# A fused spectral and MLP block on one core: block products in a fourth group, x added earlier, one subtraction moved to GpSimd

## The chip, the core and the metric

The kernel runs on one core of a Trainium2 chip. The metric is the device time of one execution, in microseconds; the time before is the median of three runs. Engines are named as the profile names them: PE (TensorE, matrix products; PEld are its weight loads), DVE (VectorE), ACT (ScalarE), POOL (GpSimd) and SP (SyncE, which here issues all the DMAs).

## The reference

Input x is 2048 x 448 in 32-bit floats. Three things are summed:

```python
xn = layernorm(x)
A  = irfft2(rfft2(xn) * (w_r + 1j * w_i))          # spectral filter, over tokens and channels
h  = gelu(xn @ w1)                                 # 448 x 448
hs = concat(h[:, quarter k] shifted by 1, -1, 2, -2 tokens) @ w2
x1 = x + hs
B  = x1 + gelu(layernorm(x1) @ w3) @ w4            # 448 x 1792, 1792 x 448
out = x + A + B
```

So x itself enters the output twice: once as the leading `x +`, once inside x1.

## The kernel before, in words

Products run in 16-bit halves: a 32-bit operand is split into a high half and a low half (the rest), and a product is three matmuls: high by high, high by low, low by high. The 2048 tokens form 16 batches of 128 (token = 16 a + b, batch b). Tile `xb(b)` holds a batch: first the normalised x, then x1 divided by the scale p12, and in the end the output.

The stages, in order of the span:

- Start (to about 113 us): loads, layernorm, first MLP products (`w1_in`, L462; `w2_mm`, L507).
- Channel MLP, eight groups G of two batches, each in seven steps fp. `front(G, fp)` (L755) makes 256 hidden columns by 22 matmuls (`mlp_in`, L433) into a PSUM bank of tag `mm`; ACT applies gelu (L763) and writes the high half of `hf` (L767), DVE the low half (L768). `back(G, fp)` (L778) multiplies `hf` by w4 into the accumulators `acc` (L798). `mlp` (L837) strings them together, with `ahead` fronts issued before each back.
- Block products (`crossed`, L752; groups listed in `STR`, which is 5, 6, 7). For the two small products, high by low and low by high, `back` uses seven products of half width (224 columns, L809) in place of eight (four 448-column matmuls), as in Strassen's scheme. That needs differences of blocks: `hg`, three DVE operations (L771 to L773) with two buffers, and `w4_forms` (L890), made once on POOL. Partial sums go to two more banks `cr` (tag `tr`), are scaled by two ACT copies (L826), combined by four POOL additions (L829) and added to the batch by two more (L833; on DVE for group 7).
- Fold (`do_fold`, L568, two batches at a time, about 113 to 190 us): SP loads raw x into `xf` (three buffers), ACT normalises it in place (L575), POOL folds it (L580 to L583), `step1_in` (L588) splits it into `xh` (L591 on ACT, L592 on DVE), `step1` (L595) transforms it (ps, L601) and splits into `y` (L605, L606).
- The filter's largest value (`w_scale`, L610): eight loads `wl` and eight DVE reductions (L268), in two buffers.
- Spectral chunks (16, about 194 to 265 us): `chunk_a` (pp, L658), `chunk_b` (px, L675; two ACT copies L680; DVE products L681 and L683 into `te`; POOL addition L685 makes z), `chunk_z` (z split: high half on ACT, L692; low half on DVE, L693), `chunk_c` (pu, L704; `y`, L707 and L708).
- Inverse (`gather_u`, `inv_a`, `inv_b`, about 270 to 380 us): per batch pe (L724), an ACT copy, two POOL and four DVE operations, a split into `vh`, py (L746), then `xb += sc * py` on DVE (L747). `finish` (L560) calls `unscaled` (L553): it loads raw x again into `xr`, computes `p12 * xb + x` on DVE (L557), and stores. Batches 12 to 15 do this earlier, in `mlp(last=True)`, into tiles `rest` in the memory `x2mem` of which their fronts have no more need.

What sets the order of the work. A scheduler places the instructions of every engine at build time, by priority: the MLP runs under `prio(FILL)`, a low priority, so that it fills PE between the transforms, and its evacuations under `prio(EVAC)`, a high one. `behind(key)` pins an instruction behind another in that order: `FOLD` lists the (G, fp) whose `hf` each fold follows, `PACE` the (G, fp) whose `back` each step1 follows, `WMAX` those of the reductions. Each engine then runs its list strictly in order, and waits at an instruction whose inputs are not there. All DMAs stand in one list on SP. PSUM banks come in four tags of two (`mm`, `tr`, `acc`, `sp`); ps, px, pu, pe and py share `sp`.

Of the kernel before, what the change touches and what calls it, by code (L numbers as in the profile page):

```python
# [31 lines left out]
AH = 2  # L32
# [3 lines left out]
WMAX = [(1, 4), (1, 5), (2, 0), (2, 0), (2, 1), (2, 2), (2, 3), (2, 4)]  # L36
LATE = [(2, 2), (2, 3), (2, 4), (2, 5)]
HS = 3
STR = (5, 6, 7)
INV, LAG = 4, 2  # L40
EVAC, FILL = 0, 100000

# [80 lines left out]
def body(tc, nc, x, wf, w1, w2, w3, w4, c_g, c_n, c_small, out):  # L123
# [434 lines left out]
        return t  # L558

    def finish(b):  # L560
        SY.dma_start(ov[:, b], unscaled(b))


    OFF = [0, 113, 225, 338, 450]
    FAM = [0, 2, 1, 3]
    folds = {}

    def do_fold(b0):  # L568
        f = pfd.tile([128, 2, 4, 113], F32, tag="xf", bufs=3, name=f"xf{b0}")
        X = f.rearrange("p b s d -> p (b s d)")[:, 0:2 * D + 2].rearrange("p (b d) -> p b d", b=2)  # L570
        after["X", b0] = (SY.dma_start(X[:, :, 0:D], xv[:, b0:b0 + 2]).ins,)
        with behind("f", *FOLD[b0 // 2]):
            for i in range(2):
                x_ = X[:, i, 0:D]
                A.activation(out=x_, in_=x_, func=AF.Identity, scale=xn_scale[b0 + i], bias=xn_bias[b0 + i])  # L575
            A.activation(out=X[:, :, D:D + 1], in_=X[:, :, 0:1], func=AF.Copy)
        ad = X[:, :, 0:D].rearrange("p b (h d) -> p h b d", h=2)[:, :, :, 0:113]
        bc = X[:, :, 1:D + 1].rearrange("p b (h d) -> p h b d", h=2)[:, ::-1, :, 223:110:-1]
        u = xr.rearrange("p (a b s d) -> p a b s d", a=2, b=2, s=2)
        P.tensor_tensor(out=u[:, 0], in0=ad, in1=bc, op=ALU.add)  # L580
        P.tensor_tensor(out=u[:, 1], in0=ad, in1=bc, op=ALU.subtract)
        for k, op in ((0, ALU.add), (2, ALU.subtract)):
            i = P.tensor_tensor(out=f[:, :, k:k + 2].rearrange("p b s d -> p s b d"), in0=u[:, :, 0], in1=u[:, :, 1], op=op)  # L583
        after["fold", b0] = (i.ins,)
        for i in range(2):
            folds[b0 + i] = f[:, i].rearrange("p s d -> p (s d)")
# [33 lines left out]
    def w_scale_end(wm):  # L620
        t = pc.tile([128, 4], F32, name="wt")
        V.tensor_reduce(out=t[:, 0:1], in_=wm, axis=AX.X, op=ALU.max)
        pt = bank("sp", "wpt")
        T.transpose(pt[0:1, 0:128], t[:, 0:1], ident)
        V.tensor_reduce(out=t[0:1, 1:2], in_=pt[0:1, 0:128], axis=AX.X, op=ALU.max)
        V.tensor_scalar(out=t[0:1, 1:2], in0=t[0:1, 1:2], scalar1=2.0 ** -20, scalar2=None, op0=ALU.max)
        pb = bank("sp", "wpb")
        T.matmul(pb[:, 0:1], ones[0:1], t[0:1, 1:2], start=True, stop=True)
        e = pc.tile([128, 3], I32, name="we")
        V.tensor_copy(out=t[:, 2:3], in_=pb[:, 0:1])  # L630
        V.tensor_single_scalar(e[:, 0:1], t.bitcast(I32)[:, 2:3], 0x7F800000, op=ALU.bitwise_and)
        V.tensor_single_scalar(e[:, 1:2], e[:, 0:1], 0x7F800000, op=ALU.bitwise_xor)
        V.tensor_scalar(out=sc[:, 0:1], in0=e.bitcast(F32)[:, 1:2], scalar1=ZPRE, scalar2=None, op0=ALU.mult)
        for h in range(2):
            V.tensor_scalar(out=sc[64 * h:64 * h + 64, 2:3], in0=sc[64 * h:64 * h + 64, 0:1], scalar1=2.0 * h - 1.0,
                            scalar2=None, op0=ALU.mult)
        V.tensor_scalar(out=sc[:, 1:2], in0=e.bitcast(F32)[:, 0:1], scalar1=2.0 ** -21 / (ZPRE * UPRE * VPRE),
                        scalar2=s12[:, 0:1], op0=ALU.mult, op1=ALU.mult)


    stream, pfs, zs = {}, {}, {}
# [46 lines left out]
    def chunk_z(c):  # L688
        z = zs.pop(c)
        zh = zb[c % 2]  # L690
        zv = [zh[:, p * 2 * DF:(p + 1) * 2 * DF] for p in range(2)]
        A.activation(out=zv[0], in_=z, func=AF.Copy)  # L692
        V.tensor_tensor(out=zv[1], in0=z, in1=zv[0], op=ALU.subtract)  # L693

    def chunk_c(c):
        _, _, k = stream.pop(c)
# [45 lines left out]
    def inv_b(b):  # L742
        vh = vhs.pop(b)
        py = bank("sp", f"py{b}")
        for n, (vi, ri) in enumerate(PASS):
            T.matmul(py[:, :D], cV[ri], vh[:, vi], start=n == 0, stop=n == 2)  # L746
        V.scalar_tensor_tensor(out=xb(b), in0=py[:, :D], scalar=sc[:, 1:2], in1=xb(b), op0=ALU.mult, op1=ALU.add)  # L747


    acc, xs, hs, hg, rest = {}, {}, {}, {}, {}  # L750
# [27 lines left out]
    def back(G, fp):  # L778
        h = hs.pop((G, fp))
        n = D // 2  # L780
        end = 4 if G == 7 else 6
        if fp == 0:
            acc[G] = [bank("acc", f"acc{G}{i}") for i in range(2)]
            if G in STR:
                xs[G] = [bank("tr", f"cr{G}{i}") for i in range(2)]
        if (G, fp) == (7, 5):
            xs[G] = [bank("tr", f"end{i}") for i in range(2)]
        C = [[(slice(0, D), acc[G][i][:, 0:D], 0, 6)] for i in range(2)]
        if G == 7:
            C[1] = [(slice(0, D), acc[G][1][:, 0:D], 0, 4)]  # L790
            if fp > 4:
                C[1] = [(slice(n * k, n * k + n), xs[G][k][:, 0:n], 5, 6) for k in range(2)]
        for i in range(2):
            for r, to, s, e in C[i]:
                with behind("m", G, fp) if (G, fp) == (7, 6) and ("m", G, fp) in after else contextlib.nullcontext():
                    for f in range(2):
                        for hi, wi in ((0, 0),) if crossed(G, fp) else ((0, 0), (0, 1), (1, 0)):
                            m = T.matmul(to, h[:, hi, 2 * f + i], w4p[0][:, wi, 2 * fp + f, r],  # L798
                                         start=fp == s and f == 0 and hi + wi == 0, stop=fp == e and f == 1 and hi == 1)
                after["m", G, fp] = (m.ins,)  # L800
        if crossed(G, fp):
            g = hg.pop((G, fp))
            X = [xs[G][k // 2][:, n * (k % 2):n * (k % 2) + n] for k in range(4)]
            H = [[acc[G][i][:, n * k:n * k + n] for k in range(2)] for i in range(2)]
            forms = [(0, 1, X[0], 9), (1, 3, H[1][0], 9), (3, 2, H[0][0], C[0][0][3]), (6, 4, X[2], 9),
                     (4, 5, X[3], end), (5, 6, X[1], end), (2, 7, H[1][1], C[1][0][3])]
            for hi, wi in ((0, 1), (1, 0)):
                for k, slot, to, e in forms:
                    m = T.matmul(to, h[:, hi, slot] if slot < 4 else g[:, hi, slot - 4], w4f[fp][k][wi], start=k in (0, 6) and fp == 0 and hi == 0,  # L809
                                 stop=hi == 1 and fp == e)  # L810
            after["m", G, fp] = (m.ins,)
        k34 = p34[:, 1:2] if G >= 6 else p34[:, 0:1]
        to = {i: rest[2 * G + i] if G >= 6 else xb(2 * G + i) for i in range(2)} if fp >= 4 else {}

        def evacuate(i):
            for r, src, _, e in C[i]:
                if fp == e:
                    V.scalar_tensor_tensor(out=to[i][:, r], in0=src, scalar=k34, in1=to[i][:, r], op0=ALU.mult, op1=ALU.add)  # L818
                    if G == 7 and fp == 6:
                        SY.dma_start(ov[:, 2 * G + i, r], to[i][:, r])  # L820

        with prio(EVAC):
            if G in STR and fp == end:
                e0, e1 = cross[:, 0], cross[:, 1]
                for i in range(2):
                    A.activation(out=cross[:, i], in_=xs[G][i][:, 0:D], func=AF.Copy, scale=k34)  # L826
                for o, x, y in ((e0[:, n:], e0[:, 0:n], e0[:, n:]), (e1[:, 0:n], e1[:, 0:n], e0[:, n:]),
                                (e0[:, n:], e0[:, n:], e1[:, n:]), (e1[:, n:], e1[:, 0:n], e1[:, n:])):
                    (V if G == 7 else P).tensor_tensor(out=o, in0=x, in1=y, op=ALU.add)  # L829
            for i in range(2):  # L830
                evacuate(i)
                if G in STR and fp == end:
                    (V if G == 7 else P).tensor_tensor(out=to[i], in0=to[i], in1=cross[:, 1 - i], op=ALU.add)  # L833
                if G == 6 and fp == 6:
                    SY.dma_start(ov[:, 2 * G + i], to[i])
# [235 lines left out]
    xh_buf = [pfd.tile([128, 2 * 452 + 16], F16, name=f"xh{i}") for i in range(4)]  # L1071
    for i in range(4):
        P.memset(xh_buf[i][:, 904:], 0.0)
    mlp([1, 2], ahead=AH, tags=("mm", "tr"))
    for b in range(0, NB, 2):
        do_fold(b)
        step1_in(b)
        step1_in(b + 1)
        with behind("m", *PACE[b // 2]):
            step1(b)  # L1080
            step1(b + 1)
# [24 lines left out]
        if 0 <= i - 3 < NC:  # L1106
            chunk_c(i - 3)
    close("pst")
    mlp(range(3, 6))
    pv = pool("pv", side="right")  # L1110
    bs = [*range(12, 16), *range(8, 12), *range(8)]
    units = [(G, fp) for G in range(4, 8) for fp in range(7)][INV:]
# [11 lines left out]
                    finish(bs[n - 1])  # L1124

    inverse(range(4))
    mlp([6], last=True)
    inverse(range(4, 17))
    mlp([7], last=True)
    for name in ("pv", "pa2", "pa", "pw", "px", "pc", "ps"):  # L1130
# [25 lines left out]
```

## Time and profile before

| | us |
|---|---|
| runs (three) | 409.61, 410.98, 411.87; median 410.98 |
| the profiled execution, its own time | 411.11 |
| its span (first to last instruction) | 409.2 |
| PE busy | 402.4 |
| DVE busy | 313.3 |
| ACT busy | 268.2 |
| POOL busy | 164.1 |

Durations below come from the one profiled execution. A busy time counts an engine as busy from the start of an instruction to its end; matmuls are pipelined, so the time that one takes of PE is read from the distance between starts, not from its own duration. In the rows, "out<-in" names tiles of the program with buffer numbers left out, "x12" is a count, and what stands in brackets behind a row is the idle time of that engine just before it and what ended it.

### The profile page before, as it was taken

What the parts mean: (1) busy time and instruction counts of PE and PEld (TensorE: products, weight loads), DVE (VectorE), ACT (ScalarE), POOL (GpSimd) and SP (SyncE); (2) the same over time, 40 slices, a digit from 0 to 9 for tenths busy, and PEclk for the clock granted to TensorE, in tenths of its full rate; (3) what the DMA queues carried; (4) which work ended last, traced back from release to release, by engine and by line L of the source; (5) the groups of instructions that cost most, each with busy time, mean ns of one, the idle gap of its engine ahead of it and who ended that gap; (6) DMA issues with size and microseconds to landing.
All of it is one profiled execution on the core that took longest, in us unless ns stands there. A gap on an engine that the chain in (4) does not pass through costs nothing.

```text
span 409.2 us, 8827 instructions
## 1 busy us (share of the span) xinstructions
PE 402.4 (98%) x3379; PEld 295.4 (72%) x3379; DVE 313.3 (77%) x674; ACT 268.2 (66%) x465; POOL 164.1 (40%) x260
## 2 busy tenths in 40 slices
PE   8999999999999999999999999999999999999996
PEld 3554555666677877677878887877788888878885
DVE  5989998898654737975899988841698969898645
ACT  4699993984838766754788888757566555644332
POOL 3889820002297745599321212100133234434300
PEclk9999999999999999999999999999999999999999
DMA  8999999907710356527367567320000202332201
GB/s 280 352 264 181 170 178 259 270 2 156 159 48 0 94 207 198 158 24 179 94 173 157 144 149 181 98 60 2 1 2 2 69 22 77 107 108 76 88 2 45
DMA packets 57209, 49.46 MB, mean 121 GB/s; under 512 B 41312, under 2 KB 52192, under 8 KB 57168
## 3 DMA queue, kind: packets, MB, share of 16 engines
q1 hardware_dynamic: 57168, 48.91, 46.3%
q8 instruction: 26, 0.43, 0.4%
q14 instruction: 15, 0.12, 0.1%
HBM read 35.06 MB, written 3.67 MB: 95 GB/s over the span
## 4 chain that ended last, share of the span: by engine, by line
PE 68%; DVE 12%; ACT 7%; DMA 6%; issue 3%; POOL 1%; SPq 0%; ACTq 0%; DVEq 0%; POOLq 0%
PE pw L433 23%; PE acc L798 18%; PE pw L462 6%; PE pw L507 6%; PE cr L809 3%; DMA wl<-wf 2%; PE acc L809 2%; ACT te L680 2%; PE ps L601 2%; PE py L746 2%; PE pe L724 2%; DVE te L683 1%; DVE te L681 1%; PE pu L704 1%; DMA h<-hs 1%
## 5 line engine op out<-in xcount | busy, mean ns | idle before, releaser
L433 PE MATMUL pw<-x2mem,w3p 128*128 128x256 f16 x1232 | 151.4, 272 | 0.0
L433 PEld LDWEIGHTS <-w3p 128*128 128x128 f16 x1232 | 118.8, 98 | 18.4
L798 PE MATMUL acc<-w4p,hf 128*128 128x448 f16 x508 | 106.7, 352 | 0.2 <-DVE xt L818 0.2
L798 PEld LDWEIGHTS <-hf 128*128 128x128 f16 x532 | 51.6, 98 | 37.1 <-issue 0.4
L768 DVE SCALAR_TENSOR_TENSOR hf<-pw,h,hf 128x512 f16<-128x512 f32 x56 | 41.8, 747 | 35.3 <-ACT hf L767 35.0
L763 ACT ACTIVATE pw<-pw,pe 128x512 f32<-128x512 f32 x56 | 36.7, 655 | 42.5 <-PE pw L433 42.4
L731 POOL TENSOR_TENSOR e<-e 128x226 f32<-128x226 f32 x16 | 12.8, 801 | 72.0 <-ACT e L728 67.9
L767 ACT ACTIVATE hf<-pw,h 128x512 f16<-128x512 f32 x56 | 38.3, 685 | 1.3
L507 PE MATMUL pw<-w2p,h 112*128 112x448 f16 x192 | 38.9, 352 | 0.1
L685 POOL TENSOR_TENSOR xr<-te 128x450 f32<-128x450 f32 x16 | 16.2, 1012 | 56.5 <-DVE te L683 50.6
L462 PE MATMUL pw<-w1p,w4x 128*128 128x448 f16 x176 | 34.9, 352 | 0.5 <-DVE h L936 0.5
L507 PEld LDWEIGHTS <-h 112*128 112x128 f16 x192 | 18.5, 98 | 16.8 <-DMA h<-x2mem 0.8
L462 PEld LDWEIGHTS <-w4x 128*128 128x128 f16 x176 | 17.0, 98 | 16.5 <-ACT w4x L422 0.7
L728 ACT ACTIVATE e<-pe 128x452 f32<-128x452 f32 x16 | 8.7, 544 | 20.7 <-PE pe L724 20.7
L580 POOL TENSOR_TENSOR xr<-xf 128x452 f32<-128x452 f32 x8 | 8.9, 1109 | 27.0 <-issue 16.0
L716 ACT ACTIVATE U<-y 113x512 f16<-113x512 f16 x32 | 18.0, 619 | 0.0
L592 DVE TENSOR_TENSOR xh<-xf,xh 128x452 f16<-128x452 f32 x16 | 14.0, 907 | 5.0 <-ACT xh L591 5.0
L680 ACT ACTIVATE te<-px 64x450 f32<-64x450 f32 x32 | 17.3, 539 | 0.6
L583 POOL TENSOR_TENSOR xf<-xr 128x452 f32<-128x452 f32 x16 | 16.7, 1066 | 0.6
L809 PE MATMUL cr<-w4x,hg 128*128 128x224 f16 x102 | 15.8, 259 | 0.1
L809 PEld LDWEIGHTS <-hg 128*128 128x128 f16 x152 | 14.7, 98 | 1.2 <-DVE hg L772 0.5
L738 ACT ACTIVATE vh<-e 128x448 f16<-128x448 f32 x16 | 9.2, 573 | 8.8 <-DVE e L736 8.8
(201 smaller groups left out, 773.1 us busy)
## 6 DMA issues: line engine op xcount, KB each, us to landing
wc<-wf SPq DMA_DIRECT2D x32, 225.0 KB, 3.7
wl<-wf SPq DMA_DIRECT2D x8, 450.0 KB, 3.7
xf<-x SPq DMA_DIRECT2D x8, 448.0 KB, 3.6
xt<-x SPq DMA_DIRECT2D x3, 896.0 KB, 11.0
w3raw<-w SPq DMA_DIRECT2D x3, 896.0 KB, 14.4
xr<-x SPq DMA_DIRECT2D x12, 224.0 KB, 2.6
out<-xr SPq DMA_DIRECT2D x12, 224.0 KB, 2.0
gn<-c_g SPq DMA_DIRECT2D x16, 128.0 KB, 3.3
```

What stands on the lines that cost most here:

```text
L433: T.matmul(ps_out, wp[:, wi + t, cols], xT[:, xi + t, tok], start=t == 0 and wi + xi == 0, stop=t == 3 and wi == 4)
L462: m = T.matmul(pm[:, :D], xTs[g][:, xi + t, 128 * i:128 * i + 128], w1p[:, wi + t], start=t == 0 and p == 0, stop=t == 3 and p == 2)
L507: m = T.matmul(w2b[b][:, :D], hT[g][:112, 4 * hi + k, o:o + 128], w2p[:, wi, k], start=k == 2 and hi + wi == 0, stop=k == 3 and hi == 1)
L583: i = P.tensor_tensor(out=f[:, :, k:k + 2].rearrange("p b s d -> p s b d"), in0=u[:, :, 0], in1=u[:, :, 1], op=op)
L680: i = A.activation(out=e[64 * h:64 * h + 64], in_=px_[64 - 64 * h:128 - 64 * h, :2 * DF], func=AF.Copy)
L685: P.tensor_tensor(out=z, in0=t[:, 0], in1=t[:, 1], op=ALU.add)
L716: A.activation(out=U[b][:113, p].rearrange("p q (c k) -> p q c k", c=NC), in_=Y1[:113, p, :, :, b], func=AF.Copy)
L763: A.activation(out=pm, in_=pm, func=AF.Gelu_apprx_tanh, scale=r3)
L767: i = A.activation(out=h[:, 0], in_=pv_, func=AF.Copy, scale=h3)
L768: j = V.scalar_tensor_tensor(out=h[:, 1], in0=pv_, scalar=h3, in1=h[:, 0], op0=ALU.mult, op1=ALU.subtract)
L798: m = T.matmul(to, h[:, hi, 2 * f + i], w4p[0][:, wi, 2 * fp + f, r], start=fp == s and f == 0 and hi + wi == 0, stop=fp == e and f == 1 a ...
L809: m = T.matmul(to, h[:, hi, slot] if slot < 4 else g[:, hi, slot - 4], w4f[fp][k][wi], start=k in (0, 6) and fp == 0 and hi == 0, stop=hi ...
```

## The change

Five edits go together.

1. `STR` becomes (4, 5, 6, 7): group 4 uses block products too.
2. In `back`, the seven half-width products are issued in two parts: first the three that need `hf` alone, for both passes, then the four that need `hg` or come last. `mlp` runs groups 3 to 5 and group 6 with two fronts ahead in place of one.
3. For batches 2 to 11 (`EARLY`), raw x is added at the fold's load: `load_fold` computes `xb = p12 * xb + X` on DVE as soon as the fold's x is there, behind (0, 6) for the first three pairs, behind the fold's own pin for the others. The scales follow: groups 1 to 5 add their MLP output with the scale for raw units, `inv_b` uses a new `sc[:, 3:4]` for these batches, and `finish` stores `xb` directly.
4. The first three fold loads are issued ahead of `mlp([1, 2])` in the program's text.
5. In `chunk_z`, the low half of z is computed on POOL.

```diff
-STR = (5, 6, 7)
+EARLY = (2, 4, 6, 8, 10)
+STR = (4, 5, 6, 7)
...
     def finish(b):
-        SY.dma_start(ov[:, b], unscaled(b))
+        SY.dma_start(ov[:, b], xb(b) if b // 2 * 2 in EARLY else unscaled(b))
...
-    def do_fold(b0):
+    Xs = {}
+
+    def load_fold(b0, pin):
         f = pfd.tile([128, 2, 4, 113], F32, tag="xf", bufs=3, name=f"xf{b0}")
         X = f.rearrange("p b s d -> p (b s d)")[:, 0:2 * D + 2].rearrange("p (b d) -> p b d", b=2)
         after["X", b0] = (SY.dma_start(X[:, :, 0:D], xv[:, b0:b0 + 2]).ins,)
+        Xs[b0] = f, X
+        if b0 in EARLY:
+            with behind("f", *pin):
+                for i in range(2):
+                    V.scalar_tensor_tensor(out=xb(b0 + i), in0=xb(b0 + i), scalar=p12, in1=X[:, i, 0:D], op0=ALU.mult, op1=ALU.add)
+
+    def do_fold(b0):
+        f, X = Xs.pop(b0)
         with behind("f", *FOLD[b0 // 2]):
...
+        V.tensor_tensor(out=sc[:, 3:4], in0=sc[:, 1:2], in1=p12, op=ALU.mult)
...
         A.activation(out=zv[0], in_=z, func=AF.Copy)
-        V.tensor_tensor(out=zv[1], in0=z, in1=zv[0], op=ALU.subtract)
+        P.tensor_tensor(out=zv[1], in0=z, in1=zv[0], op=ALU.subtract)
...
-        V.scalar_tensor_tensor(out=xb(b), in0=py[:, :D], scalar=sc[:, 1:2], in1=xb(b), op0=ALU.mult, op1=ALU.add)
+        V.scalar_tensor_tensor(out=xb(b), in0=py[:, :D], scalar=sc[:, 3:4] if b // 2 * 2 in EARLY else sc[:, 1:2], in1=xb(b),
+                               op0=ALU.mult, op1=ALU.add)
...
-            for hi, wi in ((0, 1), (1, 0)):
-                for k, slot, to, e in forms:
+            for hi, wi, part in ((0, 1, 0), (1, 0, 0), (0, 1, 1), (1, 0, 1)):
+                for k, slot, to, e in forms[3 * part:3 + 4 * part]:
...
-        k34 = p34[:, 1:2] if G >= 6 else p34[:, 0:1]
+        k34 = p34[:, 1:2] if G else p34[:, 0:1]
...
+    for b in (0, 2, 4):
+        load_fold(b, (0, 6))
     mlp([1, 2], ahead=AH, tags=("mm", "tr"))
     for b in range(0, NB, 2):
+        if b > 4:
+            load_fold(b, FOLD[b // 2])
         do_fold(b)
...
-    mlp(range(3, 6))
+    mlp(range(3, 6), ahead=AH)
...
-    mlp([6], last=True)
+    mlp([6], last=True, ahead=AH)
```

## Prediction

> **What bounds the kernel now.** I read the page first (busy time, then the chain of work that ended last), then busy time by stage, then what TensorE (PE) itself waited for.
>
> ```profile
> span 409.2 us, 8827 instructions
> ...
> PE 402.4 (98%) x3379; PEld 295.4 (72%) x3379; DVE 313.3 (77%) x674; ACT 268.2 (66%) x465; POOL 164.1 (40%) x260
> ...
> PE 68%; DVE 12%; ACT 7%; DMA 6%; issue 3%; POOL 1%; SPq 0%; ACTq 0%; DVEq 0%; POOLq 0%
> ```
>
> PE is busy for 98% of the span and carries 68% of the chain. The next view is the table of stretches: the fold (113 to 194 us from the span's start), the spectral chunks (194 to 265), group 4 (265 to 300), groups 5, 6 and the head of 7 with the inverse transform (300 to 386). Columns: bounds, length, then busy us and instruction count of PE, weight loads, VectorE (DVE), ScalarE (ACT) and GpSimd (POOL), granted clock, DMA share, GB/s.
>
> ```profile
> 113.00:194.00 81.00, 80.78 (x709) 60.05 (x708) 51.68 (x72) 51.03 (x91) 61.97 (x72) 1.00 0.42 114
> 194.00:265.00 71.00, 70.54 (x746) 57.94 (x744) 63.08 (x107) 58.33 (x107) 16.95 (x17) 1.00 0.58 143
> 265.00:300.00 35.00, 35.00 (x303) 26.17 (x301) 17.07 (x35) 21.89 (x39) 4.99 (x7) 1.00 0.08 22
> 300.00:386.00 86.00, 85.73 (x815) 71.30 (x813) 74.53 (x162) 45.63 (x80) 31.19 (x38) 1.00 0.20 65
> ```
>
> Read each row as "PE against its own length": PE is idle for 0.22, 0.46, 0.00 and 0.27 us, at a granted clock of 1.00. DVE comes next, 89% busy in the chunks and 87% in the inverse. So work taken off DVE pays only where PE waits for DVE now. The view of waits, for PE and its weight loads (us in total, times, longest):
>
> ```profile
> PE px L675 <- DVE te L681: 0.4, 2, 0.3
> PE acc L798 <- DVE xt L818: 0.2, 1, 0.2
> PE py L746 <- DVE xt L747: 0.2, 1, 0.2
> ...
> PEld L809 <- DVE hg L772: 0.5, 2, 0.3
> PEld L809 <- DVE hg L773: 0.4, 2, 0.3
> ```
>
> That is the whole reservoir behind the start-up: 0.8 us on PE and at most 0.9 us more behind its weight loads, 1.7 us in all, or 0.4% of the time. The other way to gain is to give PE fewer columns.
>
> **The change part by part.**
>
> *Group 4 as block products.* The cost of one `back` (a fourteenth of a group's second product) stands in the time between the first matmul of it and the first matmul of what follows. A plain one, then a crossed one:
>
> ```profile
> 153.78 2.43 PE L798 MATMUL acc<-w4p,hf 128*128 128x448 f16 x12
> 156.05 1.50 PE L601 MATMUL ps<-csm,xh 128*128 128x128 f16 x24
> ...
> 392.21 0.92 PE L798 MATMUL acc<-w4p,hf 128*128 128x448 f16 x4
> ...
> 394.31 2.57 PE L433 MATMUL pw<-x2mem,w3p 128*128 128x256 f16 x22
> 396.71 0.92 PE L798 MATMUL acc<-w4p,hf 128*128 128x448 f16 x4
> ```
>
> Plain: 156.05 - 153.78 = 2.27 us for 12 matmuls. Crossed: 394.31 - 392.21 = 2.10 us for 4 + 14. So 0.17 us less, in each of seven `back`s of group 4: **-1.2 us**, on PE and so on the path. (A `front`, the 22 matmuls of L433, is 396.71 - 394.31 = 2.40 us.) DVE gets three `hg` operations in each, and two ACT copies and six POOL additions come at the group's end:
>
> ```profile
> L771 DVE TENSOR_TENSOR hg<-hf 128x512 f16<-128x512 f16 x19 | 8.3, 435 | 0.4
> L773 DVE TENSOR_TENSOR hg<-hf,hg 128x256 f16<-128x256 f16 x19 | 8.2, 433 | 0.3
> L772 DVE TENSOR_TENSOR hg<-hf,hg 128x256 f16<-128x256 f16 x19 | 8.0, 419 | 0.3
> ```
>
> 7 x (0.435 + 0.433 + 0.419) = 9.0 us of DVE in a stage where it is busy 17.07 of 35.00 us: hidden. The six additions on POOL delay the inverse's first chains, whose products the order places two `back`s and two fronts later, some 9 us; hidden too.
>
> *Plain halves first, and two fronts ahead in groups 3 to 6.* The order of the changed program shows the four `hg` products of each pass behind all six that need `hf` alone, and one more front (2.4 us) between an `hf` and its use. That is aimed at the 0.9 us of weight loads that waited for `hg`, in groups 5 and 6. The price: at the turns from group 5 to 6 and 6 to 7, two `back`s now run with no front between, so py of batch 11 comes some 2 us sooner behind its pe.
>
> *Raw x at the fold.* Ten loads and ten DVE operations leave the inverse; the operations, not the loads, reappear in the fold, since the fold loads x anyway. Rows: what leaves, what POOL takes over, and DVE's old time for it.
>
> ```profile
> L557 DVE SCALAR_TENSOR_TENSOR xr<-xt,s,xr 128x448 f32<-128x448 f32 x12 | 10.3, 862 | 1.5 <-DMA xr<-x 1.4
> L693 DVE TENSOR_TENSOR zb<-xr,zb 128x450 f16<-128x450 f32 x16 | 10.5, 653 | 3.7 <-ACT zb L692 3.6
> L278 POOL TENSOR_TENSOR w2p<-w2s,w2p 112x448 f16<-112x448 f32 x2 | 2.0, 1034 | 0.0
> ```
>
> 10 x 0.862 = 8.6 us leave DVE's 74.53 in the inverse. With the ordering above I take off two thirds of that stage's waits (0.2 on PE, 0.9 on weight loads): **-0.6 us**, bounds 0 and -1.1.
>
> In the fold the 8.6 us meet a DVE busy 51.68 of 81 us, but in two places they stand in somebody's way. First, four of them now stand ahead of the first `xh`:
>
> ```profile
> 114.44 1.79 DVE L592 TENSOR_TENSOR xh<-xf,xh 128x452 f16<-128x452 f32 x2 [1.02 <-ACT xh L591]
> ...
> 118.29 1.50 PE L601 MATMUL ps<-csm,xh 128*128 128x128 f16 x24
> ```
>
> The `xh` pair ends at 116.2, and 4 x 0.862 = 3.4 us put in front of it, partly into the 1.02 us of idle time, end it near 119; the order has moved most of the first ps products behind four more front matmuls (0.4 us), so they want it near 119 too. **+0.1**, bounds 0 and +0.9. Second, the queue of loads. The order of SyncE now has all four loads of x for the last batches ahead of the last fold load and of the first filter block (wl), where one of them was:
>
> ```profile
> 147.41 0.34 SPq L556 DMA_DIRECT2D x2mem<-x  x1
> 147.92 0.37 SPq L571 DMA_DIRECT2D xf<-x  x1
> 148.38 0.89 SPq L615 DMA_DIRECT2D wl<-wf  x2
> 149.32 1.40 SPq L556 DMA_DIRECT2D x2mem<-x  x3
> ...
> xf<-x SPq DMA_DIRECT2D x8, 448.0 KB, 3.6
> ...
> xr<-x SPq DMA_DIRECT2D x12, 224.0 KB, 2.6
> ```
> ```profile
> 154.47 1.09 DVE L268 TENSOR_REDUCE wm<-wl 128x1 f32<-128x900 f32 x1 [2.24 <-DMA wl<-wf]
> ...
> 164.12 0.67 DVE L818 SCALAR_TENSOR_TENSOR xt<-acc,p,xt 128x448 f32<-128x448 f32 x1
> ```
> ```profile
> 162.06 2.56 PE L433 MATMUL pw<-x2mem,w3p 128*128 128x256 f16 x22
> 164.84 1.29 PE L798 MATMUL acc<-w4p,hf 128*128 128x448 f16 x6 [0.22 <-DVE xt L818]
> ```
>
> DVE stood 2.24 us for wl, and 9.65 us later freed the accumulator that PE was waiting for (0.22 us). Behind that reduction stand nine more DVE operations, then this evacuation, and PE behind it: each us that wl is late is a us of PE. From 2.6 us for 224 KB and 3.6 us for 448 KB, 224 KB more cost 1.0 us, so three loads more ahead make wl up to 3.0 us late; the order has moved one operation (about 0.7 us) from behind the wait to ahead of it. Bounds of this term: -0.4 (the wait goes: 162.06 to 164.84 is 2.78 us for a front of 2.40, so 0.38 start to start where the view says 0.22) and 3.0 - 0.7 = +2.3. Loads queued together overlap their fixed part, and the old queue held these transfers too, so I stay near the lower end: **+0.3**.
>
> *Low half of z by GpSimd.* DVE loses 16 x 0.653 = 10.5 of its 63.08 us in the chunks, POOL gains 16 x 1.034 = 16.5 on top of 16.95 of 71: room enough, and pu follows its z by two chunks (some 8 us), so the 0.4 us of longer latency is covered. What can be won are the two px waits, 0.4 us together. But the row before the second of them shows DVE itself idle, for ACT's copy:
>
> ```profile
> 242.59 0.69 DVE L681 SCALAR_TENSOR_TENSOR te<-px,sc,wc 128x450 f32<-128x450 f32 x1 [0.38 <-ACT te L680]
> ```
>
> ACT keeps all its work. Hence **-0.3**, bounds 0 and -0.4. There is a price that runs the other way. DVE and POOL get in each other's way when both work from SBUF:
>
> ```profile
> 338.19 1.11 DVE L772 TENSOR_TENSOR hg<-hf,hg 128x256 f16<-128x256 f16 x1
> ...
> 350.38 0.28 DVE L772 TENSOR_TENSOR hg<-hf,hg 128x256 f16<-128x256 f16 x1
> ```
> ```profile
> 337.83 2.46 POOL L833 TENSOR_TENSOR xt<-xt,x2mem 128x448 f32<-128x448 f32 x2
> ```
> ```profile
> L683 DVE SCALAR_TENSOR_TENSOR te<-te,sc,wc 128x450 f32<-128x450 f32 x16 | 10.9, 678 | 0.0
> ```
>
> The same operation took 1.11 us while POOL was adding and 0.28 alone. In the chunks the `te` product of L683 reads only SBUF. That is the third rival.
>
> The Trainium skill (SBUF — State Buffer, section "SBUF: two separate sides") says more: the port pair of VectorE and GpSimd is an exclusive lock for a whole instruction, and a VectorE operation with two SBUF inputs waits out any GpSimd operation that reads SBUF. By that rule this move costs DVE as much as it saves, and the third rival's time below would be the likelier one. The pair 1.11 and 0.28 agrees in direction; the 0.83 us between them is no more than one addition of that row (1.23 us).
>
> *Sum.* -1.2 - 0.6 + 0.1 + 0.3 - 0.3 = -1.7 us. The profiled execution took 411.11 us for a span of 409.2 (1.9 us lie around the span, and nothing in them changes). 411.1 - 1.7 = **409.4 us**, against a median of 410.98 (0.4% less).
>
> **The rivals.**
>
> *Every wait closes.* All 1.7 us of waits go and nothing comes instead: 411.1 - 1.2 - 1.7 = 408.2, and start to start they are a little longer than listed (0.38 against 0.22 above), so 407.9. For it: DVE loses 10.5 and 8.6 us in just the two stages where it is fullest. Against: ACT's 0.38 us, and a new order has waits of its own.
>
> *The filter block comes late* (slower than before). The fold's two terms at their upper bounds, +0.9 and +2.3, against -1.2 - 0.6 - 0.3: +1.1, or 412.2. It is one mechanism: DVE queued behind a later wl, PE behind DVE at the first `back` of group 2. It decides from 2.1 us in the fold on. For it: the 2.24 us and the moved loads. Against: DVE had 1.4 us and more of idle time around it.
>
> *DVE blocked by GpSimd in the chunks.* Each L683 waits out one POOL operation: 16 x 1.034 = 16.5 us more, DVE at 63.1 - 10.5 + 16.5 = 69.1 of 71 us. It still fits, but the slack of a chunk falls from 7.9 / 16 = 0.5 us to 0.1, and single px come late; at 0.1 us, the lower of the waits seen, in each of 16 chunks that is +1.6 in place of -0.3: 409.4 + 1.9 = 411.3. For it: the two rows of L772. Against: L683 is 678 ns on average today beside the z additions, no blocked one among the 16.
>
> That the edit might not do what it says is out: the order shows the 18 matmuls in group 4's `back`s, the 16 POOL operations and ten loads fewer.
>
> **How the numbers follow.** Chances: forecast 0.55, every wait closes 0.20, late filter block 0.15, blocked DVE 0.10. A difference of 0.5% is 2.05 us, about what a measurement of this kernel can tell from none. Faster by more (under 408.93): the second case and a third of the first, 0.38. Slower by more (over 413.03): the tail of the late filter block, 0.07. Same: 0.55. The forecast's own spread is 408.3 to 410.5; the range, from the closing case to the late one with 2 in 10 left out, is 407.6 to 411.8.
>
> **What would show it.** In the new profile: crossed `back`s of 2.10 us in group 4, 1.2 us less from its first to its last; no weight load waiting for `hg`; px waits of 0.1 to 0.2; the evacuation before group 2's first `back` within half a us of 164.1. It is wrong if that evacuation stands at 166 or later, if L683 rises from 0.68 to 1 us and more, or if group 4's `back`s wait for `hg` or for the additions at its end.

## The result, and the profile after

| | before | after |
|---|---|---|
| median of 22 runs each, us | 410.75 (409.61 to 412.59) | 412.21 (410.44 to 414.14) |
| ratio | | 1.0038, 95% interval 1.0027 to 1.0049 |
| the profiled execution: its own time, span, us | 411.11, 409.2 | 410.44, 408.7 |

The change makes the kernel 0.4% slower; the forecast was 0.4% faster. The profiled execution of after is the fastest of its 22 runs, 1.8 us under their median, so a typical run may wait longer than its rows show. First its head and the table of stretches, with the columns and bounds that the prediction showed for before.

```profile
span 408.7 us, 8945 instructions
...
PE 399.9 (98%) x3421; PEld 300.0 (73%) x3421; DVE 321.5 (79%) x680; ACT 268.6 (66%) x467; POOL 183.2 (45%) x282
```
```profile
113.00:194.00 81.00, 79.04 (x694) 58.97 (x693) 60.70 (x80) 50.04 (x90) 62.97 (x71) 1.00 0.38 111
194.00:265.00 71.00, 69.77 (x748) 57.89 (x746) 62.71 (x98) 58.68 (x108) 31.21 (x32) 1.00 0.58 148
265.00:300.00 35.00, 35.00 (x349) 30.51 (x347) 20.98 (x47) 22.21 (x40) 5.53 (x8) 1.00 0.07 19
300.00:386.00 86.00, 86.00 (x821) 72.23 (x819) 69.56 (x158) 45.42 (x80) 33.05 (x45) 1.00 0.10 39
```

Read each row as PE against its length again. The inverse is now without a gap (86.00 of 86), but PE idles 1.96 us in the fold, where it idled 0.22, and 1.23 in the chunks, where it idled 0.46. DVE, which was to lose 10.5 us in the chunks, went from 63.08 to 62.71. The waits of PE say for whom:

```profile
PE acc L811 <- DVE xt L831: 1.8, 1, 1.8
PE px L687 <- DVE te L693: 1.2, 5, 0.5
```

One wait of 1.8 us stands at group 2's first `back`, where there were 0.2. Five px waits, 1.2 us, stand where there were two, 0.4. The waits for `hg` and for py are gone. DVE and PE at that first `back` of group 2, in after:

```profile
156.09 2.19 DVE L269 TENSOR_REDUCE wm<-wl 128x1 f32<-128x900 f32 x2 [2.66 <-DMA wl<-wf]
...
164.60 0.68 DVE L831 SCALAR_TENSOR_TENSOR xt<-acc,p,xt 128x448 f32<-128x448 f32 x1
```
```profile
160.94 2.57 PE L434 MATMUL pw<-x2mem,w3p 128*128 128x256 f16 x22
165.33 1.29 PE L811 MATMUL acc<-w4p,hf 128*128 128x448 f16 x6 [1.82 <-DVE xt L831]
```

DVE stood 2.66 us for the filter block `wl`, and PE stood 1.82 us for the evacuation behind it.

### The profile page after: what moved, and what is told of

Its sections match the earlier page's. It is cut to its first block, busy times and chain, and to the rows that moved or that the text cites. A ratio compares the mean times of both kernels' runs of the same rounds, so it can differ in the third digit from the quotient of the medians.

```text
span 408.7 us, 8945 instructions
## 1 busy us (share of the span) xinstructions
PE 399.9 (98%) x3421; PEld 300.0 (73%) x3421; DVE 321.5 (79%) x680; ACT 268.6 (66%) x467; POOL 183.2 (45%) x282
## 4 chain that ended last, share of the span: by engine, by line
PE 45%; ACT 7%; DVE 5%; issue 3%; DMA 2%; POOL 0%; SPq 0%; DVEq 0%; ACTq 0%; POOLq 0%
PE pw L434 18%; PE acc L811 10%; PE cr L822 5%; PE acc L822 4%; ACT te L692 3%; PE pe L736 2%; DMA wl<-wf 2%; PE py L758 2%; DVE te L693 1%; PE px L687 1%; ACT x2mem L677 1%; DVE x2mem L678 1%; PE ps L612 1%; DVE te L695 1%; ACT y L719 1%
## 5 line engine op out<-in xcount | busy, mean ns | idle before, releaser
L434 PE MATMUL pw<-x2mem,w3p 128*128 128x256 f16 x1232 | 148.5, 273 | 0.0
L811 PE MATMUL acc<-w4p,hf 128*128 128x448 f16 x452 | 97.1, 352 | 1.8 <-DVE xt L831 1.8
L811 PEld LDWEIGHTS <-hf 128*128 128x128 f16 x476 | 45.9, 98 | 32.1 <-issue 2.0
L743 POOL TENSOR_TENSOR e<-e 128x226 f32<-128x226 f32 x16 | 10.7, 669 | 66.6 <-ACT e L740 61.2
L705 POOL TENSOR_TENSOR zb<-xr,zb 128x450 f16<-128x450 f32 x16 | 16.4, 1024 | 15.3 <-ACT zb L704 15.3
L822 PEld LDWEIGHTS <-hg 128*128 128x128 f16 x208 | 20.0, 98 | 0.1
L822 PE MATMUL cr<-w4x,hg 128*128 128x224 f16 x138 | 19.4, 259 | 0.0
L822 PEld LDWEIGHTS <-hf 128*128 128x128 f16 x156 | 14.9, 98 | 4.4
L603 DVE TENSOR_TENSOR xh<-xf,xh 128x452 f16<-128x452 f32 x16 | 15.5, 1009 | 3.3 <-ACT xh L602 3.3
```

The lines of the kernel that those rows point to most:

```text
L434: T.matmul(ps_out, wp[:, wi + t, cols], xT[:, xi + t, tok], start=t == 0 and wi + xi == 0, stop=t == 3 and wi == 4)
L603: j = V.tensor_tensor(out=t[:, 452:904], in0=f, in1=t[:, 0:452], op=ALU.subtract)
L705: P.tensor_tensor(out=zv[1], in0=z, in1=zv[0], op=ALU.subtract)
```

## The experiments

All times are medians, with the ratio to runs of before on the same chip (their medians lay between 410.62 and 411.19 there) and its 95% interval. PE's waits by stage come from the view of waits, cut at 113, 194 and 268 us:

| kernel | median, us | ratio to before | PE waits: fold, chunks, behind them, us |
|---|---|---|---|
| before | 410.75 | 1 | 0.2, 0.4, 0.2 (and weight loads for hg 0.9) |
| after | 412.21 | 1.0038 (1.0027 to 1.0049) | 1.8, 1.2, 0 |
| raw x at the fold alone | 413.59 | 1.0064 (1.0042 to 1.0086) | 2.4, 0.2, 0.8 |
| group 4 alone | 411.78 | 1.0014 (1.0000 to 1.0027) | 0.2, 0.5, 1.2 (and weight loads for hg 2.5) |
| order and fronts alone | 411.51 | 1.0024 (1.0011 to 1.0037) | 0.2, 0, 1.7 |
| z on GpSimd alone | 410.22 | 0.9983 (0.9971 to 0.9995) | 0.2, 0.5, 0.2 |
| group 4 with the order | 408.56 | 0.9945 (0.9925 to 0.9964) | 0.2, 0, 0 |
| after without raw x at the fold | 410.54 | 0.9975 (0.9951 to 0.9999) | 0.2, 1.3, 0.7 |
| after, filter loads first | 409.75 | 0.9977 (0.9964 to 0.9990) | 0, 1.2, 0 |

### The fold: raw x alone, and everything but it

The changed kernel with `EARLY = ()`, the other four edits kept; and before with the edits 3 and 4 alone.

> The changed kernel with raw x added at the inverse again for all batches (EARLY empty), so that the fold's DVE operations and the order of SyncE's loads are those of before. Block products in group 4, plain halves first, the fronts ahead and the low half of z on GpSimd stay. Theory F (the fold's four extra DVE operations and the later filter loads cost about 2 us at group 2's first back, and little else is wrong): the time falls to about 409.7 us (before 410.75, less 1.2 for group 4, less about 0.4 for the order, plus 0.6 for the chunks), the evacuation ahead of group 2's first back stands near 164.1 less any earlier luck, and PE waits there 0.2 us. Rival R (the loss sits in the block products or the denser PE work, with a lower granted clock): the time stays at 411.5 to 412.5. Theory C (the chunks' px waits are what costs): they stay here, 5 waits and about 1.2 us in all, and the time stays above before by about half a us.

> The kernel before with raw x added at the fold alone (the load order on SyncE and the fold's DVE order are those of the changed kernel; no block products in group 4, old order of the halves, z on DVE). Theory F: slower than before by about 1.5 us (about 2 lost at group 2's first back, 0.3 to 0.5 won in the inverse, where DVE has 8.6 us less): 412.2 us, with PE waiting 1.5 to 2 us for the evacuation near 165. Rival R: within half a us of before, 410.5 to 411.2.

Measured: 410.54 and 413.59. Without raw x at the fold the change is 0.25% faster than before (1.0 us, as expected), with it 0.38% slower: it costs 0.63%, 2.6 us, and alone as much, 0.64%. So the loss came in with raw x at the fold, and the block products do not explain it; the profiles put it at group 2's first `back`. A lower clock does not explain it either: four of the 22 runs of after had a mean granted clock of 0.994 to 0.996, and the median of the others is still 412.0. The px waits stay without raw x (1.3 us). For the run with raw x alone the expected loss, 1.5 us, was too low: it had only the profiled wait.

### Which wait in the fold: the loads of the last batches, or DVE's work

First the four loads of x for batches 12 to 15 were pinned behind the filter loads (here `after["wl"]` is set at each wl load):

```diff
-        SY.dma_start(t, xv[:, b])
+        with behind("wl") if rest_late else contextlib.nullcontext():
+            SY.dma_start(t, xv[:, b])
```

> The changed kernel with one edit: the four loads of x for the last batches are pinned behind the last filter load in SyncE's list, so that the filter blocks come first again; the fold's DVE order is that of the changed kernel. Theory F1 (of the loss in the fold the late filter load is the cause): PE waits at group 2's first back falls from 1.8 to 0.2 us and the time by 1.6 to 2 us, to about 410.5 against 411.2 of before. Rival F2 (DVE's added operations ahead of that evacuation, four before the first xh and two at each later fold, are the cause, whatever the loads do): the wait stays at 1 us or more and the time at 411.8 to 412.5.

> Both: the loads of the last batches behind the filter loads, and the low half of z on DVE. Under F1 and no interaction: the time of the run with late loads, plus or minus what the z edit gives in the run beside it; 410 to 411.2. Under F2 as much as the run with z on DVE.

Measured: 411.12, ratio 1.0025 (1.0004 to 1.0046), and with z on DVE 411.91, 1.0029 (1.0013 to 1.0045). That is 0.13% under after, and 0.17% under after with z on DVE (1.0046, below): 0.5 and 0.7 us of 2.6, and the intervals overlap. So the moved loads, the cause that the prediction named, are the smaller part by these medians; F1 as put falls, and F2 was not shown by it either. The profiled executions of these two kernels have the same order in the fold, and differ in one thing, when wl landed. With the loads late, DVE, then PE:

```profile
155.49 2.22 DVE L269 TENSOR_REDUCE wm<-wl 128x1 f32<-128x900 f32 x2 [1.33 <-DMA wl<-wf]
...
164.66 0.68 DVE L834 SCALAR_TENSOR_TENSOR xt<-acc,p,xt 128x448 f32<-128x448 f32 x1
```
```profile
165.39 1.30 PE L814 MATMUL acc<-w4p,hf 128*128 128x448 f16 x6 [1.14 <-DVE xt L834]
```

With z on DVE besides:

```profile
157.00 2.20 DVE L269 TENSOR_REDUCE wm<-wl 128x1 f32<-128x900 f32 x2 [2.89 <-DMA wl<-wf]
...
166.20 0.68 DVE L834 SCALAR_TENSOR_TENSOR xt<-acc,p,xt 128x448 f32<-128x448 f32 x1
```
```profile
166.93 1.30 PE L814 MATMUL acc<-w4p,hf 128*128 128x448 f16 x6 [2.74 <-ACT xf L589]
```

(The second wait is put down to ACT; it ends 0.05 us after DVE's evacuation, 166.20 + 0.68, and is the same one.) Here wl came 1.51 us later, the evacuation 1.54 later, PE 1.54 later: each us that wl is late is a us of PE, as the prediction had it. What was left to find was why it is late even with those loads out of the way. SyncE's list of after shows it:

```profile
146.44 1.84 SPq L557 DMA_DIRECT2D x2mem<-x  x4
149.58 0.38 SPq L574 DMA_DIRECT2D xf<-x  x1
150.01 0.94 SPq L626 DMA_DIRECT2D wl<-wf  x2
```

wl is issued 10.93 us before the front that precedes the waiting `back` (160.94), where in before it was 13.68 (148.38 and 162.06 in the prediction's rows): 2.75 us later. With raw x at the fold this lead is 10.9 us in every profile in which wl keeps its place in the list, late loads or not; without it, 13.7. From its issue to DVE's reduction, wl took as long with one of the moved loads ahead of it as with four: 154.47 - 148.38 = 6.09 us in before, 156.09 - 150.01 = 6.08 in after. So wl came late because it was issued late. It stands behind the last fold load (the code pins it behind that load), and that one waits for a buffer: it goes at 149.58, just as DVE ends the xh that last reads it (148.34 and 1.17). The chain of that fold in after, ACT and then DVE:

```profile
139.68 0.76 ACT L586 ACTIVATE xf<-xf,nm,vw 128x448 f32<-128x448 f32 x1 [1.46 <-DVE xt L579]
141.00 0.76 ACT L586 ACTIVATE xf<-xf,nm,vw 128x448 f32<-128x448 f32 x1 [0.57 <-DVE xt L579]
...
147.73 1.05 ACT L602 ACTIVATE xh<-xf 128x452 f16<-128x452 f32 x2 [2.70 <-POOL xf L594]
```
```profile
148.34 1.17 DVE L603 TENSOR_TENSOR xh<-xf,xh 128x452 f16<-128x452 f32 x2 [1.77 <-ACT xh L602]
```

and the same xh in before:

```profile
146.22 1.17 DVE L592 TENSOR_TENSOR xh<-xf,xh 128x452 f16<-128x452 f32 x2 [0.76 <-ACT xh L591]
```

ACT normalises x in place, so it must now wait until DVE has added the raw x (1.46 and 0.57 us). GpSimd folds later, ACT and DVE split later, the buffer comes free later, and through SyncE's list the filter block with it. To test this chain against DVE's own work, the first two filter loads were taken out from behind the last fold load and put two fold loads earlier. ACT's and GpSimd's lists stay the same, and DVE has as much to do:

```diff
-            SY.dma_start(h, wf.rearrange("c (p r) n -> (c p) (r n)", r=8)[:, 4 * DF * c:4 * DF * (c + 1)])
+            with behind("X", 10 if c < 2 else 14): SY.dma_start(h, wf.rearrange("c (p r) n -> (c p) (r n)", r=8)[:, 4 * DF * c:4 * DF * (c + 1)])
...
-    with behind("X", 14):
+    if True:
         wm = w_scale()
```

> The changed kernel with one edit: the first two filter loads no longer stand behind the last fold load (xf of batches 14 and 15) in SyncE's list but two fold loads earlier; ACT's and GpSimd's lists are the same as in the changed kernel, and DVE's differs in the places of the first reductions alone. Theory F3 (the added DVE operation ahead of ACT's normalisation delays the whole chain of a fold, so that the last fold buffer comes free later, so that the last fold load and the filter loads pinned behind it are issued 2 us later, and DVE waits for them ahead of group 2's first back): DVE no longer waits 2.66 us for wl, PE's wait of 1.8 us there falls to 0.2 to 0.5, and the time by 1.3 to 2.5 us, to about 410 us, below before. Rival F2 (it is the DVE time of the added operations and of operations that GpSimd slows, whatever the loads do): the evacuation is as late as now, PE waits 1 us or more, and the time stays at 411.5 to 412.5.

Measured: 409.75, ratio 0.9977 (0.9964 to 0.9990), against 1.0038 of after: 0.61%, 2.5 us. SyncE issues the two loads at 136.69, and PE goes from the front to the `back` without a wait:

```profile
136.69 0.90 SPq L626 DMA_DIRECT2D wl<-wf  x2
146.19 0.38 SPq L574 DMA_DIRECT2D xf<-x  x1
```
```profile
161.15 2.56 PE L434 MATMUL pw<-x2mem,w3p 128*128 128x256 f16 x22
163.55 1.30 PE L811 MATMUL acc<-w4p,hf 128*128 128x448 f16 x6
```

163.55 - 161.15 = 2.40, the plain front. F2 falls: DVE does all of the added work and PE waits for none of it there. Of F3 the lower part is shown, from the place of the filter loads in the queue to PE's wait. Its upper part, from ACT's new wait to the buffer, is read from the rows and was not tested by itself. Nor is all of the 2.5 us the change's own: before lost 0.38 us at this place too. The two intervals leave the gain open from about 1.8 to 3.2 us (an estimate); if it is more than the 1.8 us of the profiled wait, a wl that lands later in most runs would fit, which is not shown.

Two more kernels lengthened the wait, to see whether a long wait lowers the granted clock behind it; they reduce the first two filter blocks two and three times (`for _ in range(2 if c < 2 else 1): absmax(...)`).

> The changed kernel with the first two filter blocks reduced twice over (the same result), which puts one more reduction of 1.09 us ahead of DVE's evacuation in group 2. If the wait costs its own length and no more: 1.1 us more than the changed kernel, 413.3, with granted clocks as before the edit, and the spread of the runs as now. If a longer wait lowers the clock: more runs at 0.996 or less than the 4 in 22 of the changed kernel, and a median of 414 or more.

> The same three times over, three reductions (3.3 us) more ahead of the evacuation: PE's wait grows to about 5 us. Its own length alone: about 415.5 us. With the clock lowered behind it: most runs at 0.997 or less, a slice with a granted clock under 1 right behind the wait, and 417 or more.

Measured: 411.88, ratio 1.0031 (1.0018 to 1.0044), and 414.88, 1.0091 (1.0068 to 1.0114). The first is no slower than after, a miss on both theories: the scheduler put ten front matmuls more ahead of that `back` in PE's list, and PE waits 1.0 us there. In the second it put 19 there, and PE waits 1.7 us there and 3.5 us for ps later, in three waits of 2.0 us at most. The granted clock was 1.00 in each stretch from 113 to 386 us of both profiles; one of 18 runs had a mean of 0.996. More waiting did not bring the clock down, but the single wait did not get longer either, so the question stays open.

### Group 4 and the order of the halves

Before with `STR = (4, 5, 6, 7)` alone; with edit 2 alone; with both.

> The kernel before with one edit: group 4 among the block-product groups. By the row-based price of 0.17 us for each of seven backs, 1.2 us less than before: about 409.6 us, with group 4 free of waits for hg or 0.2 us each in a few. Rival R: no gain or a loss (410.5 to 411.5), because weight loads wait for hg in group 4 as they did in groups 5 and 6, or because the additions at the group's end come late for the inverse.

> The kernel before with plain halves first and two fronts ahead in groups 3 to 6, and nothing else. From the prediction's step: hg's waits in groups 5 and 6 go, 0.5 us less, 410.7 against 411.2. Since block products in group 4 alone gave 0.6 us more instead of 1.2 less and the three parts without the fold together gave 1.0 less, the order must be worth about 0.9 us if parts add up: 410.3. If it is worth nothing alone (411.2), it pays only with group 4, whose last backs waited 1.05 us for hg without it.

> The kernel before with block products in group 4, plain halves first and two fronts ahead, and nothing else. If the two need each other (group 4 alone waits 1.05 us for hg at its end and 0.5 more in group 6; the order alone has a late gelu output at the start of group 4, 1.2 us, and two late operations at 378 to 381 us, 1.0 us): 410.0 to 410.5, some 0.5 us less than before, since group 4's 1.2 us come and only the waits at 378 to 381 us stay. If parts simply add (plus 0.6 and plus 1.0 us): 412.5.

Measured: 411.78, 411.51 and 408.56. Each alone is no gain or a small loss (1.0014, 1.0024); together they are faster than any other part of the change, 0.9945, 2.3 us less, and faster than either expectation. Adding the parts would have given 1.0038. The work that PE saves in group 4 is there with the order and without it. In group 4 alone it is given back at the first crossed `back`s behind that group, at 304 us. PE, then DVE and GpSimd just before, in that kernel:

```profile
304.14 0.27 PE L809 MATMUL cr<-w4x,hg 128*128 128x224 f16 x1 [0.18 <-DVE hg L772]
304.94 0.27 PE L809 MATMUL acc<-w4p,hg 128*128 128x224 f16 x1 [0.53 <-DVE hg L773]
```
```profile
299.17 1.21 DVE L735 TENSOR_TENSOR e<-e 128x112 f32<-128x112 f32 x1
300.29 1.20 DVE L736 TENSOR_TENSOR e<-e 128x111 f32<-128x111 f32 x1
...
305.77 0.27 DVE L735 TENSOR_TENSOR e<-e 128x112 f32<-128x112 f32 x1
305.95 0.26 DVE L736 TENSOR_TENSOR e<-e 128x111 f32<-128x111 f32 x1
```
```profile
299.06 2.30 POOL L833 TENSOR_TENSOR xt<-xt,x2mem 128x448 f32<-128x448 f32 x2
```

The additions at the group's end run on GpSimd while the inverse's first chain and `hg` run on DVE: two operations take 1.2 us each in place of 0.27, and `hg` comes late. Two fronts ahead and the plain halves first give it the time: in the kernel with both, the same two operations are as slow (1.20 us each, at 300.43 and 301.55), and PE waits nowhere behind 268 us. That the additions are what delays `hg` is read from the rows; no run moved them. The order alone has no such work to protect, and has two late pieces of its own, gelu near group 4's start (1.0 us) and py and a low half near 380 us (0.7 us). Why it is 1.0 us slower than before is not settled by these: its PE waits come to 1.9 us, those of before to 0.8 us and 0.9 us more of weight loads.

### The low half of z

Before with it on GpSimd alone; after with it on DVE; after with the filter loads first and z on DVE.

> The kernel before with the low half of z on GpSimd alone. Theory C: ACT's te copy is put behind the copies of y and z in the order, px then waits for DVE five or so times, and some DVE operations beside GpSimd take longer: slower than before by 0.4 to 0.8 us, 411.3 us. By the prediction's term it would be 0.3 us faster, 410.5. By the lock rival (each second-stage te product waits out a GpSimd operation) L683 would average above 1 us and the time would be 412 or more.

> The changed kernel with the low half of z back on DVE. From the run of this part alone (0.17% faster, 0.7 us), the time rises to about 413 us. From the chunks' waits in the profiles (1.9 us of gaps here, 1.1 before) it would fall by 0.5, to 411.7; then the gain of that run comes from elsewhere.

> The same with the low half of z on DVE: the z edit measured once more, now without the fold's wait in the way. From the run of z alone (0.17% less) this should be 0.5 to 1 us slower than its twin with z on GpSimd; if the edit is worth nothing in the full kernel, within 0.3 us of it.

Measured: 410.22 (0.9983); 412.30, ratio 1.0046 (1.0029 to 1.0062) beside 1.0038 of after; 409.41, 0.9972 (0.9957 to 0.9988) beside 0.9977 of its twin. So the edit gains 0.7 us alone (interval 0.2 to 1.2), where a loss or 0.3 us was expected, nothing that can be told in the full kernel, and beside group 4 and the order it may cost: 0.9975 with it, 0.9945 without (the intervals overlap, and the first has edit 4 besides). Alone it took DVE's busy time in the chunks from 63.08 to 57.99 us, half of what the sixteen subtractions took; in after, `hg` operations of group 4 (3.2 us) came into that stretch besides. Where the other half went is in DVE's groups, in the chunks of after and of the kernel with group 4 and the order, where z stays on DVE (behind the count: busy us, mean ns of one, idle time before and what ended it):

```profile
L695 DVE SCALAR_TENSOR_TENSOR te<-te,sc,wc 128x450 f32<-128x450 f32 x15 | 15.1, 1006 | 0.0
```
```profile
L683 DVE SCALAR_TENSOR_TENSOR te<-te,sc,wc 128x450 f32<-128x450 f32 x14 | 9.5, 676 | 0.0
```

It rose from 0.68 to 1.01 us on average: 15.1 us in place of 15 x 0.678 = 10.2, about half of what was taken off. The rise sits in six of the sixteen products of after: each ran beside one of GpSimd's new subtractions and took 1.45 to 1.51 us, while the other ten ran beside no GpSimd work and took 0.67 to 0.68. The px waits come with another order of PE, of which these are the pu and px of one chunk in after, and in the kernel with group 4 and the order:

```profile
215.91 0.83 PE L716 MATMUL pu<-gn,zb 128*128 128x128 f16 x12
216.58 0.21 PE L670 MATMUL pp<-csm,y 113*128 113x112 f16 x1
217.30 0.74 PE L687 MATMUL px<-x2mem,gn 128*128 128x225 f16 x6 [0.51 <-DVE te L693]
```
```profile
219.04 0.83 PE L704 MATMUL pu<-gn,zb 128*128 128x128 f16 x12
...
222.27 0.74 PE L675 MATMUL px<-pf,gn 128*128 128x225 f16 x6
```

One matmul lies between them in the first, 2.4 us of other work in the second, so that the bank that px needs has been emptied. That this order is what costs was read off, not tested; z on DVE in after has three px waits of 1.1 us in all, so the GpSimd edit is not their only source.

### The best version

Group 4, the order, and the first two filter loads early; no raw x at the fold, z on DVE.

> Block products in group 4, plain halves first and the fronts ahead (0.55% faster than before when run alone), and the first two filter loads two fold loads earlier; PE's, ACT's and GpSimd's lists are the same as without the last edit. If the 0.38 us between starts that PE loses at group 2's first back in the kernel before is the filter loads' too, it goes, and the time is 0.3 to 0.5 us lower, about 408.2 against 410.8 of before. If that wait is DVE's own work, it stays, and the two early reductions may delay an xh: 408.5 to 409.5.

Measured: 408.36, ratio 0.9926 (0.9905 to 0.9947), beside 0.9945 (0.9925 to 0.9964) without the early loads; the intervals overlap. In its profile the wait at group 2's first `back` is gone, so that one was the filter loads' too. It beats both kernels: before by 0.74%, 3.0 us, and so the change as well.

## Why the prediction was wrong

**The step that failed** is the sum's term "+0.3" for the filter block, with its sentence "so I stay near the lower end". The place, the lower part of the mechanism and the price per us were right: wl late, DVE behind it, PE behind the evacuation. The term was mis-sized: 1.6 us more wait than before in the profile, 2.5 us by the run with the early loads, in place of 0.3. What made wl late was mostly not the three loads that I priced at 3.0 us: by the runs they cost 0.5 to 0.7 us, not clear of noise, and in the profiles wl landed as soon behind them as before. The change adds a wait of ACT for DVE in the folds (1.46 and 0.57 us in the rows above), which the prediction does not name. I followed DVE's added operations only to the first xh ("+0.1"), not along the later folds to the buffer, from the buffer to the last fold load, and from there to the loads pinned behind it. By the rows of the profiles this is why wl was issued 2.75 us later. The last step stands in the code, and before's rows had xf issued at 147.92 and wl right behind it, at 148.38. The upper bound, +2.3, lies near the measured size, and the rival built on it, "The filter block comes late", gave 412.2, where the median is 412.21. Both are luck: the bound is made of the wrong loads, and the rival's sum has 0.9 us at the first xh, where PE shows no wait in after, and none of the 0.8 us that the px waits rose.

**Group 4, -1.2.** Right in size; from the view of PE's instructions in after:

```profile
276.08 0.92 PE L811 MATMUL acc<-w4p,hf 128*128 128x448 f16 x4
...
278.18 2.57 PE L434 MATMUL pw<-x2mem,w3p 128*128 128x256 f16 x22
```

278.18 - 276.08 = 2.10. But "hidden too", of the six additions, holds only with edit 2: alone they delay `hg` and take the gain back. I added the two terms as if each stood by itself.

**Order and raw x in the inverse, -0.6.** The waits went altogether (1.1 us). Taking raw x out of the inverse is not needed for it: with group 4 and the order alone, that stretch has no wait either.

**z, -0.3.** The px waits rose by 0.8 us instead. The sign "if L683 rises from 0.68 to 1 us and more" came true at 1.01, and so did a part of the third rival: six of sixteen products blocked instead of each, and half of DVE's saving eaten. By the runs the edit gains 0.7 us alone and nothing that can be told in the full kernel.

**The sum by the profile** of after: -1.2 - 1.1 + 1.6 + 0.8 = +0.1 us, for a profiled execution 0.7 us under that of before, with unlike starts. With the 2.5 us that the early loads gave back, in place of the profiled 1.8, it is +0.8; of the 1.5 us between the medians some 0.7 us are not accounted for.

One sign that I had named misled: the evacuation stood at 164.60, "within half a us of 164.1", and yet 1.6 us late, since PE was there 1.1 us sooner (160.94 against 162.06). A lateness is read against the engine that waits, not against the span's start.

## What to carry to other kernels

Where an edit adds a wait inside a pipeline of buffers, follow it to the buffer's release and to everything that stands behind the next load in an in-order queue; here some 2 us of loss sat in a filter block with which the edit had nothing to do, and moving two loads out from behind that one gave it back. Edits that need each other's slack are priced together: block products without the longer lead, or the lead without them, gained nothing or lost a little, and both together gave 0.55%. Where a median lies well above the profiled run, the waits in that profile may be too small.

## What the runs showed of the hardware

- Two kernels with the same loads in the same order in the fold had the first filter block 4.70 and 6.26 us after its issue, as DVE's reduction began (150.79 and 155.49; 150.74 and 157.00). These are two single executions.
- A DVE product that reads and writes SBUF took 0.67 to 0.68 us with GpSimd idle and up to 1.51 beside it (0.68 at most over 16 in the kernel with group 4 and the order, where none ran beside GpSimd). In after:

```profile
219.87 1.51 DVE L695 SCALAR_TENSOR_TENSOR te<-te,sc,wc 128x450 f32<-128x450 f32 x1
```
```profile
219.85 1.04 POOL L705 TENSOR_TENSOR zb<-xr,zb 128x450 f16<-128x450 f32 x1 [1.04 <-ACT zb L704]
```

  They overlap for 1.02 us and the product loses 0.83 of it, so it very nearly waited the other out. The Trainium skill (SBUF — State Buffer, section "SBUF: two separate sides") calls the shared port an exclusive lock for a whole instruction; this pair agrees. The other five that were slowed lost 0.77 to 0.83 us in the same way. The cost over the stage was smaller, since ten of the sixteen met no GpSimd work.
- Of the 58 runs of after and the three kernels nearest to it with a wait of 1.1 to 2.7 us in the fold, 10 had a mean granted clock of 0.996 or less; of the 84 of eight kernels without it, none; of raw x alone, with a wait of 2.2 us, none of 6; of the 115 runs of before beside them, one. The two kernels with more reductions did not bring more of it, and no profiled run was one of these, so what lowers the clock in these runs stays open.
